# Two edits to an mLSTM and two-layer feed-forward kernel: who writes the opening's constant tiles, and where the second layer's weight decoding stands in VectorE's queue

## The chip, the cores and the metric

One core of a Trainium2 chip runs the whole program. The metric is the device time of one execution in microseconds (us). A profiled execution gives, besides its own time, a span: from the first to the last instruction of the trace. PE is TensorE's matmul side and PEld its weight loads, DVE is VectorE, ACT is ScalarE, POOL is GpSimd, and SP is the engine that only issues transfers (DMA).

## The reference

An mLSTM runs over 768 steps for 2 batches of 8 heads of width 40. Its output, 1536 tokens of 320 features, goes through two feed-forward layers of width 2048.

```python
m_new = np.maximum(f_gate[:, :, t] + m, i_gate[:, :, t])
f_stab, i_stab = np.exp(f_gate[:, :, t] + m - m_new), np.exp(i_gate[:, :, t] - m_new)
C = f_stab * C + i_stab * np.einsum('bhd,bhe->bhde', vt, kt)
n = f_stab * n + i_stab * kt
h_tilde = np.einsum('bhde,bhe->bhd', C, qt)
y[:, :, t] = sigmoid(o_gate) * h_tilde / np.maximum(np.abs(n . q), 1.0)

x = y.reshape(1536, 320)
h = x @ w_in;   x   = (h - np.tanh(h)) @ w_out        # first layer
h = x @ w_in2;  out = (h * np.tanh(softplus(h))) @ w_out2   # second layer (Mish)
```

The inputs are float32, except the weights, which come 64 bits wide and are decoded on the chip; the matrix products are made from a high and a low part of each operand.

## The kernel before, in words

**Tiling.** The 1536 tokens are 12 pieces of 128 (`order`: six chunks of each batch). The first layer takes them as 6 blocks of 2 pieces, the second as 3 blocks of 4. The hidden width 2048 is 16 slices `f` of 128. A tile of the first layer is a block and two slices, a tile of the second a block and one slice, so each is 512 columns wide. There are 48 tiles of either.

**A tile of the first layer.** `mm1` makes `h` in PSUM (L504, 16 matmuls of 256 columns), in one of three buffers of `ps_h`. `tile1` makes the activation: ACT takes two tanh, a square and a relu (L527, L528, L529, L532), DVE multiplies (`u*h`, L530), subtracts (`h-t`, L531, the last reader of the PSUM buffer) and merges (L533). `split_g` makes a high part on ACT (L143) and a low part on POOL (L517). `mm2` then adds to the accumulators of the block, 12 matmuls of 320 columns (L563, L564, L565); it stands two tiles behind `mm1`. At the end of a block's half DVE adds the accumulators into `xo` (L580).

**A tile of the second layer.** L504 makes 8 matmuls of 512 columns; ACT applies Mish twice (L544, L545) and DVE subtracts for the low part (L546, in `tile2`); then the same 12 matmuls.

**Decoding.** `conv_w(layer, f)` turns a raw weight slice into a high and a low part: DVE L180, DVE L181, ACT L182, DVE L184, ACT L187, and DVE L189 and L190 (on POOL for the first two slices). Raw slices of 704 KB are loaded by SP (L163) into three buffers; a load waits until the decoding of the slice that lay in the buffer before has ended with L190. `lead2` asks for the decodings of the second layer: the first four during the first layer's last tiles, each further one as the second layer's tiles go.

**What sets the order.** The program states an order, and a scheduler with a timing model then arranges each engine's queue; whatever it may run early it may put ahead of its place. On the chip each engine works its queue strictly in that order. `with after(x)` is the means to forbid it: an instruction traced in it stands behind those instructions of the list `x` that run on its own engine. The list `mark` holds instructions of the latest tile: in `tile1` the DVE product L530, in `tile2` the first Mish L544 on ACT alone. `lead2` traces its decodings behind `mark`.

**The opening.** Before the first weights are needed, `program` makes constant tiles: `sds` (two 128x128 indicator matrices) and `md_` (128x1024, entries 0 and -1), which the later chunks use as matmul operands for the gates, `Cst` (two state tiles of zeros), `identr` and the mask `cm`. POOL sets them (lines 621 to 648). In the same time DVE works on the gates (`gates`, L405 to L427 for the first chunk, the same scans again for the rest), ACT rounds the gate rows (`nr`, L143) and takes the exponentials of the first two chunks (`Dm`, L312), and PE multiplies the gates out (`nb`, L293 to L303) after a run of 14 matmuls (L603) that only keep it busy. Then ACT loads the sigmoid table for the output gates (L230), the exponential table again (L659), and the first decodings begin.

Of the kernel before, what the change touches and what calls it, by code (L numbers as in the profile page):

```python
# [8 lines left out]
F32 = mybir.dt.float32  # L9
F32R = mybir.dt.float32r  # L10
U32 = mybir.dt.uint32
AF = mybir.ActivationFunctionType
ALU = mybir.AluOpType
# [12 lines left out]
def kernel(  # L26
# [11 lines left out]
    nc = tc.nc  # L38
    B, P, _, HG, S = qk.shape
    H, L = 2 * HG, 128  # L40
# [5 lines left out]
    D1 = D + 1  # L46
# [42 lines left out]
    def pool(stack, name, bufs, side="left", **kw):  # L89
        return stack.enter_context(tc.tile_pool(name=name, bufs=bufs, side=side, **kw))  # L90
# [15 lines left out]
    once = pool(left, "once", 1)  # L106

    ident = const.tile([P, P], F32, name="ident")
# [11 lines left out]
    K0, KD = 2 * B, 2 * B + 2 * H  # L120
    sds = [once.tile([P, P], F32R, name=f"sd{b}") for b in range(B)]
    md_ = once.tile([P, 2, HG, L], F32R, name="md")
    dec = once.tile([P, B, HG, NCH], F32, name="dec")

    Cst = [once.tile([P, HG, 2, D1], F32, name=f"C{b}") for b in range(B)]

    last, chain, fill, mark, second = [], [], [], [], []
# [7 lines left out]
    def after(x):  # L135
        e = ExitStack()
        for i in x:
            e.enter_context(tc.issue_after(i.ins))
        return e

    def copy_r(eng, o, x):
        if eng == 0:
            nc.scalar.activation(out=o, in_=x, func=AF.Copy)  # L143
        elif eng == 1:
            nc.vector.tensor_copy(o, x)
        else:
            nc.gpsimd.tensor_scalar(o, in0=x, scalar1=1.0, scalar2=0.0, op0=ALU.mult, op1=ALU.add)
# [236 lines left out]
    identr, cm = part[:, 0], part[:, 1]  # L384
# [152 lines left out]
    def tile2(i):  # L537
        l, bi, f = tiles[i]
        nt = len(blk[l, bi]) * L
        h = hps.pop(i)  # L540
        p = late["B"]
        gh, gl = (p.tile([P, M2], F32R, tag=t, name=t, bufs=NG2)[:, 0:nt] for t in ("gh", "gl"))
        g = p.tile([P, M2], F32, tag="g2", name="g2", bufs=2)[:, 0:nt]
        mark[:] = [nc.scalar.activation(out=gh, in_=h, func=AF.Mish)]  # L544
        nc.scalar.activation(out=g, in_=h, func=AF.Mish)  # L545
        nc.vector.tensor_tensor(gl, in0=g, in1=gh.bitcast(F32), op=ALU.subtract)  # L546
        gs[i] = (gh, gl)

    def mm2(i):
# [46 lines left out]
    def program():  # L596
# [16 lines left out]
        for x in "qkqkOwOw":  # L613
# [7 lines left out]

        big = cm.bitcast(F32)
        nc.gpsimd.memset(big, 0.0)
        masked = nc.gpsimd.affine_select(
            out=cm, in_=big, pattern=[[1, L]], base=0, channel_multiplier=-1, compare_op=ALU.is_ge, fill=2.0 ** 100
        )

        for b, t in enumerate(sds):
            f = t.bitcast(F32)
            with after([masked]):  # L630
                nc.gpsimd.memset(f, 0.0)
            nc.gpsimd.affine_select(
                out=t, in_=f, pattern=[[0, P]], base=-b, channel_multiplier=1, compare_op=ALU.not_equal, fill=1.0
            )
            nc.gpsimd.affine_select(
                out=t, in_=f, pattern=[[0, P]], base=-B - b, channel_multiplier=1, compare_op=ALU.not_equal, fill=1.0
            )
        with after([masked]):
            nc.gpsimd.memset(md_.bitcast(F32), 0.0)
        mf = md_.bitcast(F32)  # L640
        for n in range(2):
            nc.gpsimd.affine_select(
                out=md_, in_=mf, pattern=[[-HG, 2], [-1, HG], [0, L]], base=-K0 - H * n, channel_multiplier=1,
                compare_op=ALU.not_equal, fill=-1.0,
            )
        with after([masked]):
            for t in Cst:
                nc.gpsimd.memset(t, 0.0)
        copy_r(0, identr, ident)
        for n, v_ in enumerate((-G_T,)):  # L650
            nc.vector.memset(bias[:, n:n + 1], v_)
        nc.vector.memset(ones, 1.0)
# [107 lines left out]
        seg_at, k = {}, 0  # L760
# [21 lines left out]
        for i in range(len(tiles)):  # L782
            l, bi, f = tiles[i]
            if i == n_s:
                fill.clear()
            if l == 0 and i in seg_at:
                k = seg_at[i]
# [21 lines left out]
            if l == 0:  # L809
                tile1(i)  # L810
                if not i:
                    session(2, NCH)
                qm.append(i)
                if len(qm) > LAG:
                    mm2(qm.pop(0))
                if i:
                    ahead(int(14 * (k + (i - i0 + 1) / n_seg + 0.4)))
                if k >= T2:
                    next(sg, None)
                    next(sg, None)  # L820
            else:
                tile2(i)
                qm.append(i)
                if len(qm) > LAG2:
                    mm2(qm.pop(0))
                next(sg, None)
        while qm:
            mm2(qm.pop(0))

    ones = const.tile([BH, HP], F32, name="ones")  # L830
    program()


# [59 lines left out]
```

## Time and profile before

| | |
|---|---|
| median of 3 runs | 472.6 us (472.59 to 474.25) |
| the profiled execution | 472.48 us, of which the trace's span is 470.4 us |
| mean granted TensorE clock | 0.992 |
| PE busy | 455.7 us (97% of the span) |
| weight loads | 412.7 us (88%) |
| DVE busy | 321.7 us (68%) |
| ACT busy | 284.1 us (60%) |
| POOL busy | 121.2 us (26%) |

The busy shares of the page tell where the work is. The 40 slices of the page, 11.8 us each, tell where PE has holes and where its granted clock fell. The chain of waits tells which engine the end depends on in each stretch. The timeline lists instructions in order of time, with the idle time before one and what ended it in brackets. PE's matmuls are pipelined and their ends are modelled, so its idle time is best read as the distance of two starts less the usual distance for so many matmuls.

### The profile page before, as it was taken

What the parts mean: (1) busy time and instruction counts of PE and PEld (TensorE: products, weight loads), DVE (VectorE), ACT (ScalarE), POOL (GpSimd) and SP (SyncE); (2) the same over time, 40 slices, a digit from 0 to 9 for tenths busy, and PEclk for the clock granted to TensorE, in tenths of its full rate; (3) what the DMA queues carried; (4) which work ended last, traced back from release to release, by engine and by line L of the source; (5) the groups of instructions that cost most, each with busy time, mean ns of one, the idle gap of its engine ahead of it and who ended that gap; (6) DMA issues with size and microseconds to landing.
All of it is one profiled execution on the core that took longest, in us unless ns stands there. A gap on an engine that the chain in (4) does not pass through costs nothing.

```text
span 470.4 us, 8021 instructions
## 1 busy us (share of the span) xinstructions
PE 455.7 (97%) x3103; PEld 412.7 (88%) x3103; DVE 321.7 (68%) x544; ACT 284.1 (60%) x513; POOL 121.2 (26%) x132
## 2 busy tenths in 40 slices
PE   9969989999999999999999998999999999999996
PEld 5636879999989999999999887999989888998995
DVE  8998999989876888666889887899942211221111
ACT  2979646685674865888887675877643323332331
POOL 9412536355363331342433333000000000000000
PEclk9997999999999999999999999999999999999999
DMA  7784462613505121000120110255301000010001
GB/s 246 269 325 128 143 190 81 216 49 109 156 5 173 35 63 63 1 1 1 63 63 0 63 57 7 75 176 181 123 1 56 2 0 1 0 57 0 1 0 56
DMA packets 22745, 38.04 MB, mean 81 GB/s; under 512 B 1364, under 2 KB 17044, under 8 KB 22708
## 3 DMA queue, kind: packets, MB, share of 16 engines
q1 hardware_dynamic: 22708, 37.54, 24.3%
q8 instruction: 24, 0.39, 0.4%
q14 instruction: 13, 0.11, 0.1%
HBM read 35.41 MB, written 1.97 MB: 79 GB/s over the span
## 4 chain that ended last, share of the span: by engine, by line
PE 74%; DVE 11%; issue 6%; ACT 4%; DMA 2%; POOL 2%; ACTq 0%; DVEq 0%; POOLq 0%; SPq 0%
PE h L504 32%; PE acc L563 10%; PE acc L565 10%; PE acc L564 10%; PE sc L329 4%; PE pv L349 3%; POOL gl L517 2%; DMA raw<-in_w_dram 2%; PE it L338 1%; PE xt L254 1%; DVE raw L181 1%; DVE raw L180 1%; PE st L370 1%; DVE g L530 1%; DVE t L531 1%
## 5 line engine op out<-in xcount | busy, mean ns | idle before, releaser
L504 PE MATMUL h<-xT,w 128*128 128x256 f32 (+1 forms) x1152 | 212.2, 324 | 7.1 <-ACT w L187 2.3
L504 PEld LDWEIGHTS h<-xT,w 128*128 128x128 f32 x1152 | 169.7, 190 | 24.8 <-ACT w L187 2.8
L563 PE MATMUL acc<-w,gh 128*128 128x320 f32 x384 | 119.4, 313 | 1.2 <-ACT gh L143 0.6
L564 PE MATMUL acc<-w,gh 128*128 128x320 f32 x384 | 118.0, 309 | 0.0
L565 PE MATMUL acc<-w,gl 128*128 128x320 f32 x384 | 109.9, 311 | 0.0
L517 POOL TENSOR_TENSOR gl<-g,gh 128x512 fp32r<-128x512 f32 x48 | 66.0, 1375 | 140.9 <-ACT gh L143 129.6
L546 DVE TENSOR_TENSOR gl<-g,gh 128x512 fp32r<-128x512 f32 x48 | 33.1, 690 | 85.7 <-ACT g L545 85.7
L563 PEld LDWEIGHTS acc<-w,gh 128*128 128x128 f32 x384 | 72.2, 188 | 5.0 <-issue 1.3
L544 ACT ACTIVATE gh<-h 128x512 fp32r<-128x512 f32 x48 | 28.6, 597 | 75.7 <-PE h L504 75.6
L564 PEld LDWEIGHTS acc<-w,gh 128*128 128x128 f32 x384 | 72.2, 188 | 2.1
L565 PEld LDWEIGHTS acc<-w,gl 128*128 128x128 f32 x384 | 69.5, 188 | 1.8 <-issue 0.4
L533 DVE COPY_PREDICATED g<-u,t 128x512 f32<-128x512 uint32 x48 | 41.0, 853 | 7.7 <-ACT u L532 7.5
L143 ACT ACTIVATE gh<-g 128x512 fp32r<-128x512 f32 x48 | 30.4, 633 | 23.8 <-DVE g L533 20.2
L530 DVE TENSOR_TENSOR g<-u,h 128x512 f32<-128x512 f32 x48 | 32.6, 680 | 16.1 <-ACT u L529 9.5
L532 ACT ACTIVATE u<-u,bias 128x512 f32<-128x512 f32 x48 | 34.8, 725 | 9.4 <-DVE g L530 9.2
L527 ACT ACTIVATE u<-h 128x512 f32<-128x512 f32 x48 | 28.3, 591 | 16.1 <-PE h L504 16.1
L187 ACT ACTIVATE w<-raw 128x704 fp32r<-128x704 f32 x32 | 27.5, 866 | 15.1 <-DVE raw L184 15.0
L184 DVE SCALAR_TENSOR_TENSOR raw<-raw 128x704 uint32<-128x704 uint32 x32 | 32.2, 1009 | 2.8 <-ACT raw L182 2.6
L182 ACT ACTIVATE raw<-raw 128x704 f32<-128x704 f32 x32 | 27.5, 864 | 10.0 <-DVE raw L181 9.0
L531 DVE TENSOR_TENSOR t<-h,t 128x512 f32<-128x512 f32 x48 | 32.8, 683 | 0.0
L529 ACT ACTIVATE u<-u 128x512 f32<-128x512 f32 x48 | 30.4, 634 | 0.0
L181 DVE SCALAR_TENSOR_TENSOR raw<-raw 128x704 uint32<-128x704 uint32 x32 | 30.0, 940 | 0.3
(105 smaller groups left out, 506.1 us busy)
## 6 DMA issues: line engine op xcount, KB each, us to landing
raw<-in_w_dram SPq DMA_DIRECT2D x32, 704.0 KB
qk_t<-in_qk_dram SPq DMA_DIRECT2D x12, 512.0 KB
kv_t<-in_kv_dram SPq DMA_DIRECT2D x12, 324.0 KB
out_dram<-xo SPq DMA_DIRECT2D x12, 160.0 KB
xo<-in_og_dram SPq DMA_DIRECT2D x2, 640.0 KB
xo<-in_og_dram SPq DMA_DIRECT2D x2, 320.0 KB
sd<-nr SPq DMA_DIRECT2D x20, 4.0 KB
md<-nr SPq DMA_DIRECT2D x10, 8.0 KB
```

Of the source, the lines that this page charges most:

```text
L181: nc.vector.scalar_tensor_tensor(lo32, in0=z, scalar=0x80000000, in1=lo32, op0=ALU.bitwise_and, op1=ALU.bitwise_or)
L184: third[layer, f] = nc.vector.scalar_tensor_tensor(z, in0=z, scalar=3, in1=lo32, op0=ALU.logical_shift_left, op1=ALU.bitwise_or)
L504: y = nc.tensor.matmul(t[:, k * nt:(k + 1) * nt], lhsT=w[:, o:o + P], rhs=x[:, kk, :], start=(n == 0), stop=(n == len(pairs) - 1),)
L517: nc.gpsimd.tensor_tensor(gl, in0=g, in1=gh.bitcast(F32), op=ALU.subtract)
L530: mark[:] = [nc.vector.tensor_tensor(g, in0=u, in1=h, op=ALU.mult)]
L531: nc.vector.tensor_tensor(t, in0=h, in1=t, op=ALU.subtract)
L532: nc.scalar.activation(out=u, in_=u, func=AF.Relu, bias=bias[:, 0:1])
L533: nc.vector.copy_predicated(out=g, mask=u.bitcast(U32), data=t)
L546: nc.vector.tensor_tensor(gl, in0=g, in1=gh.bitcast(F32), op=ALU.subtract)
L563: nc.tensor.matmul(a, lhsT=gh[:, sl], rhs=wh, start=(f in ends_), stop=False)
L564: nc.tensor.matmul(a, lhsT=gh[:, sl], rhs=wl, start=False, stop=False)
L565: nc.tensor.matmul(a, lhsT=gl[:, sl], rhs=wh, start=False, stop=(f + 1 in ends_ or f == NF - 1))
```

## The change

The constant tiles of the opening are no longer set by POOL. DVE adds columns of the identity matrix into `picks` (two short additions), and ACT copies a column of it over each tile (`sds`, and `md_` with scale -1); the zeros of `Cst` are copied by ACT from a constant. In `tile2` the list `mark` also gets DVE's subtraction L546, so that a decoding of the second layer that `lead2` traces behind a second-layer tile stands behind that tile's L546 in DVE's queue, as it did behind L544 in ACT's.

```diff
     def tile2(i):
         mark[:] = [nc.scalar.activation(out=gh, in_=h, func=AF.Mish)]
         nc.scalar.activation(out=g, in_=h, func=AF.Mish)
-        nc.vector.tensor_tensor(gl, in0=g, in1=gh.bitcast(F32), op=ALU.subtract)
+        mark.append(nc.vector.tensor_tensor(gl, in0=g, in1=gh.bitcast(F32), op=ALU.subtract))
...
-        masked = nc.gpsimd.affine_select(
+        nc.gpsimd.affine_select(
             out=cm, in_=big, pattern=[[1, L]], base=0, channel_multiplier=-1, compare_op=ALU.is_ge, fill=2.0 ** 100
         )
+        picks = once.tile([P, H + B, 1], F32, name="picks")
+        for n, (k, d, w_) in enumerate(((K0, H, H), (0, B, B))):
+            nc.vector.tensor_tensor(
+                picks[:, H * n:H * n + w_, 0], in0=ident[:, k:k + w_], in1=ident[:, k + d:k + d + w_], op=ALU.add
+            )
+        copy_r(0, identr, ident)
+        nc.scalar.activation(
+            out=md_.rearrange("p r g s -> p (r g) s"), in_=picks[:, 0:H].to_broadcast([P, H, L]), func=AF.Copy, scale=-1.0
+        )
         for b, t in enumerate(sds):
-            f = t.bitcast(F32)
-            with after([masked]):
-                nc.gpsimd.memset(f, 0.0)
-            nc.gpsimd.affine_select(out=t, in_=f, ...)
-            nc.gpsimd.affine_select(out=t, in_=f, ...)
-        with after([masked]):
-            nc.gpsimd.memset(md_.bitcast(F32), 0.0)
-        mf = md_.bitcast(F32)
-        for n in range(2):
-            nc.gpsimd.affine_select(out=md_, in_=mf, ...)
-        with after([masked]):
-            for t in Cst:
-                nc.gpsimd.memset(t, 0.0)
-        copy_r(0, identr, ident)
+            copy_r(0, t, picks[:, H + b].to_broadcast([P, P]))
+        zero = nc.const_aps.tensor(0.0, [P, HG * 2 * D1], F32)
+        for t in Cst:
+            copy_r(0, t.rearrange("p g r d -> p (g r d)"), zero)
```

The queues move in two places. The first is the start of POOL's and of ACT's queue, in the opening (`C_98`, `C_99` are the state tiles, `n_101` holds `identr` and the mask, `sd_94`, `sd_95` and `md` are the indicators). POOL's:

```order
 L623 MEMSET n_101 128x128
 L624 AFFINE_SELECT n_101<-n_101 128x128
-L631 MEMSET sd_94 128x128
-L631 MEMSET sd_95 128x128
-L639 MEMSET md 128x1024
-L648 MEMSET C_98 128x328
-L648 MEMSET C_99 128x328
-L632 AFFINE_SELECT sd_94<-sd_94 128x128
-L632 AFFINE_SELECT sd_95<-sd_95 128x128
-L642 AFFINE_SELECT md<-md 128x1024
-L635 AFFINE_SELECT sd_94<-sd_94 128x128
-L635 AFFINE_SELECT sd_95<-sd_95 128x128
```

Eleven instructions (the last, a second L642, follows these) leave POOL between the mask and `dl`. ACT's queue in the same place:

```order
 L609 ACT_TABLE_LOAD
 L609 ACTIVATE scr<-const-float32-0.0 128x1
+L143 ACTIVATE C_98<-const-float32-0.0 128x328
+L143 ACTIVATE C_99<-const-float32-0.0 128x328
 L143 ACTIVATE n_101<-ident 128x128
+L634 ACTIVATE md<-picks 128x1024
+L143 ACTIVATE sd_94<-picks 128x128
+L143 ACTIVATE sd_95<-picks 128x128
 L312 ACTIVATE Dm<-nb 128x512 x2
```

Five copies come in ahead of the first exponentials. PE's queue and SP's are the same in the opening, and DVE's gets the two short additions before its wait for the first gate rows.

The second place is DVE's queue at the end of the first layer. Before, the last tiles of that layer stand like this; `raw_3513` is the raw slice f=6 of the second layer, and `g_3340`, `g_3383` and `g_3430` are the activations of the last three tiles:

```order
L531 TENSOR_TENSOR t_3339<-h_3321,t_3339 128x512
L180 TENSOR_SCALAR raw_3513<-raw_3513 128x704
L533 COPY_PREDICATED g_3340<-u_3338,t_3339 128x512
L530 TENSOR_TENSOR g_3383<-u_3381,h_3364 128x512
L531 TENSOR_TENSOR t_3382<-h_3364,t_3382 128x512
L181 SCALAR_TENSOR_TENSOR raw_3513<-raw_3513 128x704
...
L533 COPY_PREDICATED g_3383<-u_3381,t_3382 128x512
L530 TENSOR_TENSOR g_3430<-u_3428,h_3411 128x512
L531 TENSOR_TENSOR t_3429<-h_3411,t_3429 128x512
L533 COPY_PREDICATED g_3430<-u_3428,t_3429 128x512
L546 TENSOR_TENSOR gl_3500<-g2_3501,gh_3499 128x512
L184 SCALAR_TENSOR_TENSOR raw_3014<-raw_3014 128x704
```

In the changed program the last two tiles of the layer are `g_3368` and `g_3415`, and the raw slices f=4, 5 and 6 are `raw_2999`, `raw_3212` and `raw_3498`:

```order
L533 COPY_PREDICATED g_3368<-u_3366,t_3367 128x512
L580 SCALAR_TENSOR_TENSOR xo_91<-acc_3292,xo_91 128x256
L580 SCALAR_TENSOR_TENSOR xo_91<-acc_3292,xo_91 128x128
L533 COPY_PREDICATED g_3415<-u_3413,t_3414 128x512
...
L546 TENSOR_TENSOR gl_3485<-g2_3486,gh_3484 128x512
L180 TENSOR_SCALAR raw_2999<-raw_2999 128x704
L546 TENSOR_TENSOR gl_3510<-g2_3511,gh_3509 128x512
L180 TENSOR_SCALAR raw_3212<-raw_3212 128x704
L181 SCALAR_TENSOR_TENSOR raw_2999<-raw_2999 128x704
L546 TENSOR_TENSOR gl_3535<-g2_3536,gh_3534 128x512
L180 TENSOR_SCALAR raw_3498<-raw_3498 128x704
```

The first two passes (L180, L181) of the slices f=4, 5 and 6 of the second layer stood among the first layer's tiles (those of `raw_3014` and `raw_3227` further ahead than the rows show) and now stand behind the first second-layer subtractions L546. With them the scheduler has arranged the matmuls of PE and the passes of ACT in that stretch anew; the work is the same.

## Rows read from the trace of the kernel before

**Rows 1.** Chain of waits, opening: start, length (us), engine, tile, line.

```profile
3.73 1.20 DVE n L410
...
5.56 1.06 DVE n L427
...
8.98 0.99 DVE gg L412
...
11.56 0.74 ACT nr L143
...
13.08 1.09 ACT Dm L312 x2
...
63.12 0.41 PE xt L254 x2
```

**Rows 2.** Timeline, opening: start, busy us, instruction, count, idle before it.

```profile
3.28 0.96 POOL L639 MEMSET md<- 128x1024 f32 x1
3.34 0.28 DVE L408 TENSOR_TENSOR gi<-gi,gF 16x128 f32<-16x128 f32 x1
...
8.06 1.28 ACT L312 ACTIVATE Dm<-nb 128x512 f32<-128x512 f32 x2 [5.57 <-PE nb L303]
...
8.19 1.75 POOL L642 TENSOR_SCALAR_AFFINE_SELECT md<-md 128x1024 fp32r<-128x1024 f32 x1
...
11.60 0.45 PE L303 MATMUL nb<-n 128*128 128x512 f32 x1
```

**Rows 3.** Timeline of DVE, end of the first layer.

```profile
265.22 0.53 DVE L180 TENSOR_SCALAR raw<-raw 128x704 uint32<-128x704 uint32 x1 [1.15 <-DMA raw<-in_w_dram]
...
283.17 0.53 DVE L180 TENSOR_SCALAR raw<-raw 128x704 uint32<-128x704 uint32 x1 [2.13 <-DMA raw<-in_w_dram]
```

**Rows 4.** Chain of waits, second layer: PE's steady pace.

```profile
455.42 1.85 PE h L504 x8
...
459.04 1.85 PE h L504 x8
```

**Rows 5.** Timeline of PE, end of the first layer and first tiles of the second.

```profile
259.43 2.10 PE L504 MATMUL h<-xT,w 128*128 128x256 f32 x16
261.87 0.38 PE L563 MATMUL acc<-w,gh 128*128 128x320 f32 x1 [0.34 <-DVE xo L580]
...
267.28 0.30 PE L565 MATMUL acc<-w,gl 128*128 128x320 f32 x1
268.15 0.41 PE L563 MATMUL acc<-w,gh 128*128 128x320 f32 x1 [0.56 <-ACT gh L143]
...
271.80 0.31 PE L565 MATMUL acc<-w,gl 128*128 128x320 f32 x1
272.77 2.14 PE L504 MATMUL h<-xT,w 128*128 128x256 f32 x16 [0.66 <-DVE t L531]
275.00 0.39 PE L563 MATMUL acc<-w,gh 128*128 128x320 f32 x1
...
284.25 0.31 PE L565 MATMUL acc<-w,gl 128*128 128x320 f32 x1
285.68 2.05 PE L504 MATMUL h<-xT,w 128*128 128x512 f32 x8 [1.11 <-DVE t L531]
287.90 0.39 PE L563 MATMUL acc<-w,gh 128*128 128x320 f32 x1 [0.17 <-DVE xo L580]
```

**Rows 6.** Timeline of DVE, second layer: decodings.

```profile
301.17 0.29 DVE L190 TENSOR_TENSOR w<-raw,w 64x128 fp32r<-64x128 f32 x1
...
306.03 0.90 DVE L181 SCALAR_TENSOR_TENSOR raw<-raw 128x704 uint32<-128x704 uint32 x1
...
312.27 0.29 DVE L190 TENSOR_TENSOR w<-raw,w 64x128 fp32r<-64x128 f32 x1
...
342.84 0.29 DVE L190 TENSOR_TENSOR w<-raw,w 64x128 fp32r<-64x128 f32 x1
```

**Rows 7.** Timeline of PE, second layer: last matmuls of slice f=4.

```profile
303.62 1.32 PE L504 MATMUL h<-xT,w 128*128 128x512 f32 x5
```

More of the change, by code (lines that the diff above doesn't have):

```diff
@@ L623, in program @@
         nc.gpsimd.memset(big, 0.0)
-        masked = nc.gpsimd.affine_select(
+        nc.gpsimd.affine_select(
             out=cm, in_=big, pattern=[[1, L]], base=0, channel_multiplier=-1, compare_op=ALU.is_ge, fill=2.0 ** 100
         )
-        for b, t in enumerate(sds):
-            f = t.bitcast(F32)
-            with after([masked]):
-                nc.gpsimd.memset(f, 0.0)
[L632 to L637, printed above, removed]
-        with after([masked]):
-            nc.gpsimd.memset(md_.bitcast(F32), 0.0)
-        mf = md_.bitcast(F32)
-        for n in range(2):
[L642 to L645, printed above, removed]
-        with after([masked]):
-            for t in Cst:
-                nc.gpsimd.memset(t, 0.0)
-        copy_r(0, identr, ident)
+        picks = once.tile([P, H + B, 1], F32, name="picks")
[7 more added lines that the diff above has]
+        )
+        for b, t in enumerate(sds):
+            copy_r(0, t, picks[:, H + b].to_broadcast([P, P]))
+        zero = nc.const_aps.tensor(0.0, [P, HG * 2 * D1], F32)
+        for t in Cst:
+            copy_r(0, t.rearrange("p g r d -> p (g r d)"), zero)
         for n, v_ in enumerate((-G_T,)):
```

## The prediction, made before the run

> **What bounds the kernel now.** I read the chain of waits first, because PE is busy in nearly the whole span and a busy share says nothing of which microsecond counts. The reader is to see that the chain has two kinds of stretch. From the first gate rows up to 63 us it runs through DVE and ACT alone, and only there does it pass to PE [rows 1]. PE is busy in that time too, but largely with fillers. So whatever shortens the DVE and ACT sequence before 63 us brings everything behind it forward. From 63 us to the end the chain is PE's, and there only a hole in PE's sequence costs time.
>
> For the holes I went to PE's timeline, since its idle brackets understate them: a matmul's modelled end covers part of a wait. In the second layer a tile takes 459.04 - 455.42 = 3.62 us, of which 1.85 for the h matmuls [rows 4]; the 12 matmuls into accumulators take the other 1.77, so 0.15 each. A first-layer h tile has 16 matmuls of half the width, the same columns, and so 1.85 as well. Distances between starts above this are lost. Six of them stand at the end of the first layer [rows 5]: 261.87 - 259.43 - 1.85 = 0.59; 268.15 - 267.28 - 0.15 = 0.72; 272.77 - 271.80 - 0.15 = 0.82; 275.00 - 272.77 - 1.85 = 0.38; 285.68 - 284.25 - 0.15 = 1.28; 287.90 - 285.68 - 1.85 = 0.37. Together 4.2 us. Gaps of about 0.1 at other changes between h and accumulators add up to some 0.8 more, an estimate. I found no such hole in the second layer until the last matmul.
>
> What ends these waits is DVE: t of L531, which frees an h buffer, the sums of L580, which free an accumulator, and g, from which ACT makes gh [rows 5]. And DVE itself, in the same stretch, sits idle in front of a decoding pass whose raw slice has not landed: 1.15 us before 265.22 and 2.13 us before 283.17 [rows 3]. Those slices are f=5 and f=6 of the second layer. DVE works its queue in order, so L533 and the next L530 and L531 stand still behind them.
>
> **The change, part by part.**
>
> *POOL loses eleven instructions in the opening.* Nothing waits for their results soon; what they cost is DVE's time. L410 took 1.20 us while POOL set md and the tiles behind it, L427 took 1.06, and L412, a copy of five columns, 0.99 while POOL's L642 ran [rows 1, 2]. DVE's L408, on as many elements as L410 and in the middle of POOL's memset of md, took 0.28 [rows 2]. I take 0.28 for each of the three without POOL: 0.92 + 0.78 + 0.71 = 2.4 us less on DVE until n_all is ready, 9.1 instead of 11.5. That is the upper bound of this part; nothing gained is the lower, in case the passes are slow for another reason.
>
> *What is late next.* ACT's two roundings nr began at 11.56 and lead to the Dm of the second piece at 13.08 [rows 1]. They would start when the first Dm ends, at 8.06 + 1.28 = 9.34 [rows 2], and take the same 13.08 - 11.56 = 1.52 us, until 10.9. But the second piece's Dm needs PE's last L303 of the gate products, which ends at 11.60 + 0.45 = 12.05 [rows 2], and PE gets there after a run of fillers and matmuls without a hole, which the change leaves alone. One exponential of a pair takes 1.28 / 2 = 0.64 or less, so the pair ends at about 12.65 instead of 13.08 + 1.09 = 14.17 [rows 1]. **Gain 1.5 us.** I take this value rather than 2.4 because the L303 row is a bound that stays. From there the sigmoid's table load, the sigmoids and the first decodings follow on ACT and DVE alone, so the 1.5 us should come through to 63 us. The loads that this sequence needs are issued by SP as their buffers come free, so they move with it.
>
> *ACT gains five copies, DVE two additions.* ACT waited 5.57 us before the first Dm [rows 2]; that is the cover. By the row, a 512-wide activation costs at most 0.64, so md (1024) costs at most 1.28, and the two state tiles and the two sd at most 0.64 each: 3.84, hidden with 1.7 us to spare. identr, which L303 needs, now stands behind the zeros, and so 1.28 us later at most, in the same wait. The additions go into DVE's wait for the gate rows. Cost: nothing. The Trainium skill speaks against this step: "ScalarE: Activation LUTs", Rules for kernel authors, gives additions and multiplications to VectorE rather than ScalarE, and its section on the table load puts an activation at 186 ns and 0.833 ns per column, by which the five would take an estimated 2.5 us. By that too they stay inside the wait; the rule matters only if the cover is gone, which is a rival below.
>
> *The second layer's early passes go behind L546.* In DVE's queue the first two passes of f=4, 5 and 6 leave the end of the first layer, and with them the two waits for a load of 1.15 and 2.13 us [rows 3] and three times 0.53 + 0.90 = 1.43 us of work [rows 3, 6], 4.3 us. With 1.15 + 2.13 + 4.3 = 7.6 us less in front of it, DVE's share of a tile (L530, L531, L533, L580) follows PE instead of holding it. Following the new order with the durations above, I find h buffers freed 2 to 4 us before PE asks, and no wait for gh or gl over a few tenths. The bounds: nothing gained, if the rearranged queues bring waits of their own, and 4.2 + 0.8 = 5.0, all of the holes. I take the six holes, **4.2 us**, and leave the small gaps, which are changes between kinds of matmul as much as waits.
>
> *What the moved work costs later.* DVE has the 4.3 us to do after the first L546. In the second layer POOL is idle and DVE nearly full: from the end of f=7 to that of f=15 eight decodings took 342.84 - 312.27 = 30.57 us, 3.82 each [rows 6], against PE's 3.62 [rows 4]. It lives on a lead. Before, f=4 was decoded at 301.17 + 0.29 = 301.46, and PE came for its low part at 303.62 [rows 6, 7], a lead of 2.2 us. After, DVE enters the layer sooner by what it no longer waits for; I count a lead of over 3 us at f=4 and about 2 at f=15. Cost: nothing, if that holds.
>
> **Sum.** The profiled execution took 472.48 us, 0.12 below the median of the three runs, 472.6. 472.48 - 1.5 - 4.2 = **466.8 us**, 1.2% under the median. About 0.5%, 2.4 us, can be told from no change here.
>
> **The rivals.**
> 1. *The opening gains nothing.* For it: PE's fillers are sized to this opening, and loads fill it. Against it: the chain of waits shows no transfer and no PE between the first Dm and 63 us. 472.48 - 4.2 = 468.3.
> 2. *Half of the head's gain is given back.* The new order runs two or three h tiles in a row and puts two tiles of DVE passes together; a wait for gl from POOL or for an accumulator can take the place of a wait for h. 472.48 - 1.5 - 2.1 = 468.9.
> 3. *The edit of mark brings nothing at the head*: the waits pass to the rearranged ACT queue. 472.48 - 1.5 = 471.0.
> 4. *PE waits for decodings in the second layer* (the other side). DVE enters the layer no sooner, because its last passes wait for ACT and for accumulators. Then f=4 comes 4.3 us later than before, 2.1 us after PE; and with no lead left each of the eleven slices f=5 to f=15 costs 3.82 - 3.62 = 0.2, 2.2 us. It decides from the point at which L190 of f=4 ends later than PE's first h matmul of f=4 plus four. With the opening's gain: 472.48 - 1.5 + 4.3 = 475.3.
> 5. *ACT is late with the copies.* If they took over 5.6 us, half as much again as the bound above, the first Dm moves: every us over is a us, and the opening's gain is gone after 1.5. At 1 us net loss, 472.48 + 1.0 - 4.2 = 469.3.
>
> **How the numbers follow.** The forecast has 0.56, rival 1 0.14, rival 2 0.12, rival 3 0.07, rival 4 0.09, rival 5 0.02. Faster by over 0.5% (under 470.2): the forecast and rivals 1, 2 and 5, 0.84, less 0.01 for their edge, 0.83. Rival 3 and a third of rival 4 with that edge make 0.11 for within 0.5%, and the rest of rival 4, 0.06, is slower (over 475.0). The forecast's own range is 465.2 (both parts nearly at their upper bounds, 0.9 and 0.8 more, would be 465.1) to about 468. To hold 8 in 10 the range must reach rivals 1 and 2: 465.2 to 469.6.
>
> **What would show it.** Opening: L410, L427 and L412 near 0.3 us, n_all ready near 9, the sigmoid's table load at about 12.7 instead of 14.2, and the chain's passage to PE near 61.6. If L410 stays over 1 us, the first step is wrong; if the table load comes earlier and 63 us does not, the way onward is. End of the first layer: no DVE idle in front of L180 among the tiles, and starts of PE there at 1.85 and 0.15 without holes. If holes remain, the engine named in front of them is rival 2 or 3. Second layer: L190 of f=4 ends over 2 us before PE needs it, and PE shows no wait for DVE or ACT on weights; if it does, rival 4. The forecast is wrong if the time lies over 468.5 with both mechanisms in place, for then PE was held by something that neither part names.

## The result, and the profile after

The changed kernel takes 469.01 us (median of 4 runs, 468.47 to 469.83) against 473.21 for the kernel before (4 runs beside them): ratio 0.9909, 95% interval 0.9886 to 0.9931, so 4.2 us or 0.9% faster. It lies inside the predicted range, 2.2 us above the predicted time. The profiled execution took 468.47 us, its span is 466.5 us (before: 472.48 and 470.4), at a mean granted clock of 0.991.

**Opening.** The timeline of DVE in the changed kernel (start, busy us, engine, instruction) answers to [rows 1]:

```profile
3.74 0.21 DVE L410 TENSOR_SCALAR n<-gi 16x128 fp32r<-16x128 f32 x1
...
4.89 0.28 DVE L427 TENSOR_TENSOR n<-n_all,n 32x128 fp32r<-32x128 f32 x1
...
7.46 0.15 DVE L412 COPY gg<-gF 16x5 f32<-16x5 f32 x1
7.65 1.54 DVE L413 TENSOR_TENSOR_SCAN n_all<-gg,n_all,gi 16x640 f32<-16x640 f32 x1
```

The three passes are short and n_all is ready at 9.19. ACT's timeline of the same stretch:

```profile
2.21 0.83 ACT L143 ACTIVATE C<-const-float32-0.0 128x328 f32<-128x328 f32 x2
...
3.14 1.04 ACT L634 ACTIVATE md<-picks 128x1024 fp32r<-128x1024 f32 x1
4.08 0.49 ACT L143 ACTIVATE sd<-picks 128x128 fp32r<-128x128 f32 x2
7.31 1.27 ACT L312 ACTIVATE Dm<-nb 128x512 f32<-128x512 f32 x2 [2.74 <-PE nb L303]
...
11.96 1.28 ACT L230 ACT_TABLE_LOAD   x1
```

The five copies take 2.4 us and leave 2.74 us of waiting before the first Dm, which begins earlier than before (7.31 against 8.06 in [rows 2]). The sigmoid's table load begins 2.2 us earlier. In ACT's timeline of the kernel before it stood behind the Dm of [rows 1]:

```profile
14.19 1.28 ACT L230 ACT_TABLE_LOAD   x1
```

In the changed kernel the chain of waits names a different engine at the start:

```profile
0.84 4.90 PE w_ps L603 x14
...
18.73 0.37 PE st L370 x9
...
20.40 0.86 ACT raw L182
...
61.26 0.41 PE xt L254 x2
```

PE's fillers head the chain now, and PE holds it until 19.1 us; then it runs through ACT and DVE, and it comes back to PE at 61.26, not 63.12 [rows 1]. So 1.9 us of the 2.2 arrive there.

**End of the first layer.** From 225 to 300 us DVE has no wait for a raw slice in front of L180, where it had 1.15 and 2.13 us [rows 3] and, for f=4 before 246.67, a further 1.31. Of PE's six holes [rows 5] none is left in its place; one new one has come, here in the timelines of PE, DVE and POOL:

```profile
266.51 3.62 PE L504 MATMUL h<-xT,w 128*128 128x256 f32 x29
270.96 0.39 PE L563 MATMUL acc<-w,gh 128*128 128x320 f32 x1 [0.83 <-DVE xo L580]
```

```profile
267.85 1.79 DVE L184 SCALAR_TENSOR_TENSOR raw<-raw 128x704 uint32<-128x704 uint32 x1
269.56 0.75 DVE L533 COPY_PREDICATED g<-u,t 128x512 f32<-128x512 uint32 x1
270.19 1.15 DVE L580 SCALAR_TENSOR_TENSOR xo<-acc,xo 128x256 f32<-128x256 f32 x4
```

```profile
267.59 1.30 POOL L517 TENSOR_TENSOR gl<-g,gh 128x512 fp32r<-128x512 f32 x1 [2.82 <-ACT gh L143]
```

29 matmuls of 1.85 / 16 each would be 3.35 us, and the next begins 4.45 after: 1.1 us lost. PE waits for an accumulator that L580 empties, and L580 stands behind the third pass L184 of a decoding, which takes 1.79 us in place of 0.88. That is about what is left of POOL's L517 when it begins (1.04, until 268.89) and then its own length, 1.92 together.

**Second layer.** PE now waits for weights, which it did not do before:

```profile
320.21 1.20 PE L504 MATMUL h<-xT,w 128*128 128x512 f32 x4 [0.23 <-ACT w L187]
...
331.92 1.20 PE L504 MATMUL h<-xT,w 128*128 128x512 f32 x4 [0.23 <-ACT w L187]
```

By the distance of starts these two lose 0.39 us each; two more before 324.18 and 335.91 lose 0.23 and 0.26. Together 1.3 us. DVE's timeline and the chain of waits say why:

```profile
297.07 0.29 DVE L190 TENSOR_TENSOR w<-raw,w 64x128 fp32r<-64x128 f32 x1
...
298.98 0.29 DVE L190 TENSOR_TENSOR w<-raw,w 64x128 fp32r<-64x128 f32 x1
...
301.50 0.53 DVE L180 TENSOR_SCALAR raw<-raw 128x704 uint32<-128x704 uint32 x1 [0.65 <-DMA raw<-in_w_dram]
...
305.14 0.53 DVE L180 TENSOR_SCALAR raw<-raw 128x704 uint32<-128x704 uint32 x1 [1.59 <-DMA raw<-in_w_dram]
305.59 0.89 DVE L184 SCALAR_TENSOR_TENSOR raw<-raw 128x704 uint32<-128x704 uint32 x1
...
309.48 0.29 DVE L190 TENSOR_TENSOR w<-raw,w 64x128 fp32r<-64x128 f32 x1
...
340.20 0.29 DVE L190 TENSOR_TENSOR w<-raw,w 64x128 fp32r<-64x128 f32 x1
```

```profile
299.35 5.77 DMA raw<-in_w_dram
```

The load of slice f=8 starts when the decoding of f=5 has left its buffer (298.98 + 0.29 = 299.27), takes 5.77 us, and DVE waits 1.59 us for it; L184 at 305.59, the next pass of f=7, stands behind that wait. In the kernel before, the same two slices waited too, but less, 0.73 us for f=7 and 0.41 for f=8:

```profile
303.34 0.29 DVE L190 TENSOR_TENSOR w<-raw,w 64x128 fp32r<-64x128 f32 x1
...
308.40 0.53 DVE L180 TENSOR_SCALAR raw<-raw 128x704 uint32<-128x704 uint32 x1 [0.41 <-DMA raw<-in_w_dram]
```

From the end of f=5 to L180 of f=8 were 308.40 - 303.63 = 4.77 us, and now are 305.14 - 299.27 = 5.87. Why this load is 1.1 us longer, no run shows; the loads of f=7, f=8 and f=9 overlap in both kernels. The lead of the decoding over PE, from the end of L190 to PE's matmuls on the low part, is seen in PE's timelines of the changed kernel (f=4, the first four of the eight matmuls, and f=7) and of the kernel before (f=7):

```profile
299.26 2.01 PE L504 MATMUL h<-xT,w 128*128 128x512 f32 x8
...
310.31 1.10 PE L504 MATMUL h<-xT,w 128*128 128x512 f32 x4
```

```profile
314.23 1.10 PE L504 MATMUL h<-xT,w 128*128 128x512 f32 x4
```

At f=4 it is 299.26 - 297.36 = 1.9 us (2.2 before), at f=7 310.31 - 309.77 = 0.5 us (314.23 - 312.56 = 1.7 before). From f=7 to f=15 a decoding takes (340.20 - 309.48) / 8 = 3.84 us, more than PE's 3.62 [rows 4], so the rest of the lead is soon gone; the first wait, at 320.21, is for f=10. The last decoding ends at 340.49, only 2.6 us earlier than before (342.84 + 0.29 in [rows 6]), while PE entered the layer nearly 5 us earlier (1.7 and 3.1 us, worked out in the point-by-point part).

### The profile page after: what moved, and what is told of

It is laid out like the page before. It is cut to its first block, busy times and chain, and to the rows that moved or that the text cites. A ratio compares the mean times of both kernels' runs of the same rounds, so it can differ in the third digit from the quotient of the medians.

```text
span 466.5 us, 8014 instructions
## 1 busy us (share of the span) xinstructions
PE 454.3 (97%) x3103; PEld 412.5 (88%) x3103; DVE 317.0 (68%) x546; ACT 286.7 (61%) x518; POOL 113.4 (24%) x121
## 3 DMA queue, kind: packets, MB, share of 16 engines
q1 hardware_dynamic: 22708, 37.54, 24.7%
## 4 chain that ended last, share of the span: by engine, by line
PE 69%; DVE 15%; issue 7%; ACT 5%; POOL 2%; DMA 1%; POOLq 0%; ACTq 0%; DVEq 0%; SPq 0%
PE h L504 28%; PE acc L565 9%; PE acc L563 9%; PE acc L564 9%; PE sc L329 4%; PE pv L349 4%; DVE raw L184 3%; POOL gl L517 2%; DVE raw L181 2%; DVE raw L180 2%; DVE gl L546 2%; PE it L338 2%; DVE w L189 1%; DVE w L190 1%; PE w_ps L603 1%
## 5 line engine op out<-in xcount | busy, mean ns | idle before, releaser
L563 PE MATMUL acc<-w,gh 128*128 128x320 f32 x384 | 118.4, 312 | 0.8 <-DVE xo L580 0.8
L565 PE MATMUL acc<-w,gl 128*128 128x320 f32 x384 | 108.7, 311 | 0.0
L517 POOL TENSOR_TENSOR gl<-g,gh 128x512 fp32r<-128x512 f32 x48 | 65.5, 1365 | 135.4 <-ACT gh L143 131.0
L546 DVE TENSOR_TENSOR gl<-g,gh 128x512 fp32r<-128x512 f32 x48 | 33.2, 691 | 87.1 <-ACT g L545 87.0
L544 ACT ACTIVATE gh<-h 128x512 fp32r<-128x512 f32 x48 | 28.7, 597 | 77.1 <-PE h L504 74.2
L563 PEld LDWEIGHTS acc<-w,gh 128*128 128x128 f32 x384 | 72.1, 188 | 3.3 <-ACT w L187 1.0
L527 ACT ACTIVATE u<-h 128x512 f32<-128x512 f32 x48 | 28.4, 593 | 16.6 <-PE h L504 16.6
L184 DVE SCALAR_TENSOR_TENSOR raw<-raw 128x704 uint32<-128x704 uint32 x32 | 32.2, 1006 | 3.1 <-ACT raw L182 3.0
L181 DVE SCALAR_TENSOR_TENSOR raw<-raw 128x704 uint32<-128x704 uint32 x32 | 28.7, 899 | 0.3
```

What stands on the lines that cost most here:

```text
L181: nc.vector.scalar_tensor_tensor(lo32, in0=z, scalar=0x80000000, in1=lo32, op0=ALU.bitwise_and, op1=ALU.bitwise_or)
L184: third[layer, f] = nc.vector.scalar_tensor_tensor(z, in0=z, scalar=3, in1=lo32, op0=ALU.logical_shift_left, op1=ALU.bitwise_or)
L517: nc.gpsimd.tensor_tensor(gl, in0=g, in1=gh.bitcast(F32), op=ALU.subtract)
L546: mark.append(nc.vector.tensor_tensor(gl, in0=g, in1=gh.bitcast(F32), op=ALU.subtract))
L563: nc.tensor.matmul(a, lhsT=gh[:, sl], rhs=wh, start=(f in ends_), stop=False)
L565: nc.tensor.matmul(a, lhsT=gl[:, sl], rhs=wh, start=False, stop=(f + 1 in ends_ or f == NF - 1))
```

## The experiments

Each ratio is to runs of the kernel before on the same chip. The changed kernel's own ratio is 0.9909.

### The two edits alone

`e_open`: the change without its line in `tile2`.

```diff
-        mark.append(nc.vector.tensor_tensor(gl, ...))
+        nc.vector.tensor_tensor(gl, ...)
```

> The kernel before with the edit of the opening alone; the queues of PE and SP are those of the kernel before. Theory: the opening is worth 1.5 us and up to 2.2 if PE's fillers finish as early as in the changed kernel's profile (5.7 us instead of 6.4). Sigmoid's table load at 12.0 to 12.7 instead of 14.19, everything at 63 us 1.2 to 1.9 earlier, of which 1.5 to 1.7 is left at 245 us; the six holes of PE at the end of the first layer (4.2 us) and DVE's two waits for raw slices stay. So 473.2 - 1.5 = 471.7 us, ratio 0.996 to 0.997. Rival A (the opening's gain is given back in the first layer, where PE already waits for DVE): 63 us earlier, 285 us not, 473 us. Rival B (the two edits help one another): the holes shrink too, since DVE has more lead, and the time is below 470.5 us.

Measured: 471.4 us, ratio 0.9968 (0.9956 to 0.998), so 1.5 us, with an interval from 0.9 to 2.1. The time is the theory's, and both rivals' times are out. Where the gain lies is not shown, because the profiled execution is the odd one of the last section, with PE at about half its pace; only DVE's opening can be read from it, and there L410, L427 and L412 take 0.21, 0.28 and 0.15 us as in the changed kernel.

`e_mark`: the kernel before with that line alone.

```diff
-        nc.vector.tensor_tensor(gl, ...)
+        mark.append(nc.vector.tensor_tensor(gl, ...))
```

> The kernel before with the edit of mark alone; the queues of PE and SP are those of the changed kernel, the opening is that of the kernel before (table load at 14.2). Theory: the rearranged end of the first layer saves about 3.3 us of PE's holes, and the second layer gives back 1.2 to 1.3 us in waits for weights decoded by ACT and DVE, in both cases whatever the opening does: 473.2 - 2.1 = 471.1 us, ratio 0.995 to 0.996. Its sum with the opening alone is then the whole change (-4.2). Rival A (the head's gain needs the lead that the opening gives DVE): within 0.8 us of before, above 472.4. Rival B (the waits in the second layer come from the opening being earlier, loads being too late): then they are absent here and the time is below 470.3 us.

Measured: 471.28 us, ratio 0.9967 (0.9955 to 0.9979), so 1.6 us. The table load stands at 14.19. The hole before L563 (0.83 in brackets, 1.09 lost) and the waits for weights (0.52, 0.26, 0.38, 0.26 us) are nearly those of the changed kernel, so neither depends on the opening; rivals A and B are out. The two parts by ratio give 0.9968 x 0.9967 = 0.9935 against 0.9909. The missing 1.2 us are no larger than the intervals of the three ratios together allow. But 1.0 us of them is in this profile. PE's timeline, and the table by stretch (busy us of PE, PEld, DVE, ACT and POOL with their instructions, then the granted clock, the DMA share and GB/s):

```profile
16.20 1.08 PE L349 MATMUL pv<-kv_t,Dm 128*128 128x41 f32 x8 [0.18 <-DVE Dm L331]
...
17.60 1.74 PE L349 MATMUL pv<-kv_t,Dm 128*128 128x41 f32 x8
```

```profile
15.00:20.00 5.00, 4.78 (x32) 3.48 (x32) 4.64 (x11) 4.20 (x7) 1.05 (x2) 0.78 0.66 181
20.00:25.00 5.00, 5.00 (x34) 2.25 (x33) 3.88 (x9) 3.33 (x8) 2.28 (x2) 0.53 1.05 403
```

PE came early (fillers of 4.83 us) and waited for DVE's Dm. Then the granted clock was 0.50, the 1.2 GHz level, from about 17.8 to 24.7 us (by the table 2.2 us of the first stretch and 4.7 of the second), and the same eight matmuls take 1.74 us instead of 1.08. The first tanh L527 begins at 31.24 against 30.26 in the profile before, 1.0 us late. From there on this kernel saves 2.0 us of the span (470.4 to 469.4), as the changed kernel does (3.9 us of the span, of which it has 1.9 by the first tanh, at 28.34).

### POOL beside DVE

`e_dead`: POOL works on an unread tile, in short instructions.

```diff
...
+        dead = once.tile([P, 2 * L], F32, name="dead")
+        with after([masked]):
+            for _ in range(8):
+                nc.gpsimd.memset(dead, 0.0)
+        for _ in range(9):
+            nc.gpsimd.affine_select(out=dead, in_=dead, pattern=[[0, 2 * L]], ...)
```

> The changed kernel with POOL kept busy again in the opening, by 8 memsets and 9 affine selects on a tile that nobody reads; the result does not change, and PE's and SP's queues are those of the changed kernel. Theory (it is POOL's work beside DVE that made the short DVE passes long): L410 back to 1.0 us or more, L427 too if an affine select runs beside it, n_all ready 1.5 us or more later than 9.19, the sigmoid's table load at 13.2 or later instead of 11.96, and the time 1.2 to 1.7 us above the changed kernel, about 470.4 us (ratio to before 0.994). Rival A (the passes were long because their operands came from POOL, or because of what ACT and PE did at the time): L410 and L427 stay at 0.2 to 0.3, the time stays at 469.0 us. Rival B (PE's fillers set the opening): the passes get long but the table load comes only 0.7 us later or less, and the time is within 0.7 us of the changed kernel.

Measured: 471.08 us (469.31 to 472.0), ratio 0.9954 (0.9939 to 0.9968). L410 took 0.30, L427 0.28, L412 0.36; the table load stood at 12.34, 0.4 us late. The theory as written missed. The time is over rival A's as well: in this profile PE waits 0.26 and 0.32 us for Dm near 16 and 17.5, and the granted clock is then 0.79 in 15 to 20 us and 0.53 in 20 to 25, as in `e_mark`. The eleven executions fall in two groups: four took 469.31 to 469.61 us at a mean granted clock of 0.989 to 0.991, seven took 470.89 to 472.0 at 0.983 to 0.989. The first group is within 0.6 us of the changed kernel's median, so what POOL's short instructions cost by themselves is small.

`e_dead3`: three memsets of 128x1024 in place of those seventeen.

```diff
...
+        dead = xp.tile([P, 2 * WC], U32, tag="x", name="dead", bufs=NB - 1).bitcast(F32)
+        with after([masked]):
+            for _ in range(3):
+                nc.gpsimd.memset(dead[:, 0:2 * HG * L], 0.0)
```

> The changed kernel with three memsets of 128x1024 put back on POOL behind the mask, on a tile that nobody reads; PE's and SP's queues and every other engine's are those of the changed kernel. The run before this one used short POOL instructions (256 columns), and L410 took only 0.30 us beside them. Theory (a DVE pass of the kinds of L410, L427 and L412 waits until the POOL instruction then running has ended, so that long POOL instructions cost and short ones don't): L410, which begins at 3.7 inside a memset of 0.96 us, ends with the end of a memset (3.9, 4.9 or 5.8 us), 0.5 to 2.1 us long; L427 too if it begins before 5.8; n_all ready 0.7 to 2 us later than 9.19; sigmoid's table load at 12.5 to 13.5 instead of 11.96. Time 0.5 to 1.5 us above the changed kernel's 469.0. Rival (long or short, POOL beside DVE costs nothing, and in the kernel before it was the operands that came late): L410 at 0.2 to 0.3, time 469.0.

Measured: 469.92 us, ratio 0.9944 (0.993 to 0.9958); table load at 12.83, which its fillers of 5.78 us explain (next group); n_all was ready at 9.36, only 0.2 us late, so the theory's size missed. DVE's passes, then POOL's:

```profile
3.72 0.29 DVE L410 TENSOR_SCALAR n<-gi 16x128 fp32r<-16x128 f32 x1
...
4.61 0.41 DVE L422 CAST n<-n_all 128x128 fp32r<-128x128 f32 x1
5.06 0.28 DVE L427 TENSOR_TENSOR n<-n_all,n 32x128 fp32r<-32x128 f32 x1
```

```profile
2.98 2.98 POOL L631 MEMSET dead<- 128x1024 f32 x3
```

The first two memsets end at 3.94 and 4.95. L410 ends at 4.01 and L422 (0.23 alone) at 5.02, each just behind one; L427, inside the third, is not held at all. In `e_dead` it is the same on a smaller scale: L410 ends at 4.10 behind a memset that ends at 4.03, and L412 at 7.89 behind a select that ends at 7.87. So a pass does wait for the end of a POOL instruction, but here only for the rest of one, and not every pass does. "SBUF — State Buffer" of the Trainium skill, in "SBUF: two separate sides", says that GpSimd and VectorE share a pair of ports, held by one for a whole instruction, and that a VectorE operation with two SBUF inputs is shut out only by a GpSimd operation that reads SBUF. The runs agree: L427 has two inputs, takes 0.28 inside a memset and 1.06 beside a select [rows 1].

`e_dead4`: all eleven old instructions, on an unread tile, with dl behind them.

```diff
...
-            copy_r(2, dl, Dm[:, :, L - 1:L])
+            with after(deads):
+                copy_r(2, dl, Dm[:, :, L - 1:L])
...
+            for n in (P, P, 2 * HG * L, HG * 2 * D1, HG * 2 * D1):
+                nc.gpsimd.memset(dead[:, 0:n], 0.0)
+        for n in (P, P, 2 * HG * L, P, P, 2 * HG * L):
+            deads.append(nc.gpsimd.affine_select(out=dead[:, 0:n], ...))
```

> The changed kernel with all eleven POOL instructions of the kernel before put back, in the old order and sizes (five memsets, six affine selects), but on a tile that nobody reads, and dl behind them. The scheduler arranges later tiles anew, so only the first 20 us are read. Theory (POOL's instructions beside DVE, memsets and above all affine selects, hold some DVE passes until the running POOL instruction ends, whoever reads the tiles): the old picture returns, L410 1.0 to 1.2 us, L427 about 1.0, L412 about 1.0, n_all ready at 11.5 and the sigmoid's table load at 14.2, 1.5 to 2.2 us later than in the changed kernel's profiles (11.96 to 13.0). Rival (the old passes waited on their operands, which shared a tile or a counter with what POOL wrote): the passes stay at 0.15 to 0.4 us as in the two runs with POOL work so far, and the table load at 12 to 13.

```profile
3.72 0.81 DVE L411 TENSOR_SCALAR n<-gi 16x128 fp32r<-16x128 f32 x1
...
13.40 1.28 ACT L230 ACT_TABLE_LOAD   x1
```

L410 (L411 here) is back at 0.81, L427 took 0.39, L412 0.25, n_all was ready at 10.74 and the table load came 1.4 us late. That lies between the theory and the rival. Of the 2.3 us that n_all moved from before to the changed kernel (11.53 to 9.19) 1.55 return, without anyone reading the tiles: POOL's work as such makes DVE late. But only half of the return is in the three passes of the prediction (0.60, 0.11 and 0.10 more than in the changed kernel). Most of the rest is in two others, L408 of the later chunks (1.48 against 0.81) and L422 (0.50 against 0.23). That L427 and L412 were long before for the same reason is not shown by this run; in the trace before, L412 ends at 9.97 [rows 1], 0.03 us behind POOL's select L642 [rows 2], as it does in `e_dead`. Why the other 0.8 us did not return is open. One difference is in the traces: before, each of POOL's instructions began before the last had ended (at 4.17, where the memset of md ends at 4.24 [rows 2]), and L410 ended at 4.93, behind the last memset (4.86); here they stand some 0.05 us apart, and L411 ended at 4.53, behind the memset that was running (4.46). (The whole, 478.35 us, is not compared: PE stands still for 1.94 us before 14.59, DVE makes the Dm that PE needs only from 13.81 on, behind L180 and L181 of a decoding, and the granted clock is 0.50 from 15 to 25 us.)

### PE's fillers

`before_again`: the kernel before, unchanged.

> The kernel before once more, for a second profile of it. In the profiles so far PE's 14 opening fillers took 4.83 to 4.90 us in three kernels and 5.65 or 5.66 in two others, with no order in it that follows the edits. Theory (this belongs to the execution, not to the kernel): the fillers may take either here; if 4.9, the first Dm begins near 7.3 instead of 8.06 but the sigmoid's table load stays at 14.19, set by DVE and ACT, PE waits for DVE's Dm of L331 between 15 and 18 us, and a granted clock under 1.00 follows, as with the edit of mark alone; the time is then 473.0 to 474.0 us. If 5.66, everything is as in the profile before, 472.4 to 472.8 us. Rival (the edit of the opening speeds the fillers up): they take 5.6 us or more here in any case and the time does not differ with it.

Measured: 472.77 us, fillers 6.12 us, table load 14.18. That is a third value, and with it ten profiles of kernels with these 14 fillers show 4.62 to 6.12 us, in no order of the edits: before 5.66, with the line in `tile2` alone 4.83, the changed kernel 4.90, `e_pool` 5.65. With the new opening and nothing added on POOL the table load follows them: 4.90 and 11.96, 5.65 and 12.71, 5.89 and 12.94, 5.96 and 13.00, always 7.04 to 7.06 apart. With the old one it is 14.18 or 14.19 at 4.83, 5.66 and 6.12. So the cap of the prediction is real, and the rival (the edit speeds the fillers up) is out, because the fillers are short in a kernel without that edit (4.83) and long in others with it (5.65 to 5.96).

`e_fill10`: the changed kernel with fewer fillers.

```diff
-        spin(14)
+        spin(10)
```

> The changed kernel with 10 fillers instead of 14 at PE's start; the scheduler arranges later parts of the queues anew. In the profiles with the new opening the sigmoid's table load stands at 11.96 where the fillers took 4.90 us and at 12.71 to 13.00 where they took 5.65 to 5.96. Theory (with DVE out of the way PE's fillers and gate products are the last to come, the cap of the prediction): with four fillers fewer PE is ready at 5.2, when L427 ends, and the table load comes at 11.9 to 12.2 whatever the clock; 0 to 1 us is gained, on average 0.5: 468.5 us. Rival A (with fewer fillers the clock rises later, and the gate products run at half speed): the table load at 12.5 or later, no gain. Rival B (the rearranged queues decide): the opening is earlier, but the time is over 469.5 us.

```profile
0.84 4.42 PE L603 MATMUL w_ps<-const-bfloat16-1.0 128*32 128x512 bf16 x10 [0.84 <-PEq L874]
```

The table load came at 11.78, as the theory says. But the exponential's load behind it came at 15.29, later than the 14.63 of the changed kernel, because ACT waits 0.72 us between the two sigmoids for the transfer of the output gates, which the changed kernel does not. At the first tanh (28.68 against 28.34) nothing was left. Three executions, with the profiled one, took 469.3, 469.44 and 471.52 us, ratio 0.9941 (0.9919 to 0.9962): no gain. Three more took 476.47 to 477.08 at a mean granted clock of 0.973, where the others had 0.985 to 0.996; no profile shows where the clock fell in them.

### The lead in the second layer

`e_pool`: the last two passes of f=7 to 15 on POOL.

```diff
-        eng = nc.gpsimd if layer == 0 and f < PRE else nc.vector
+        eng = nc.gpsimd if layer == 0 and f < PRE or layer == 1 and f >= 7 else nc.vector
```

> The changed kernel with L189 and L190 of the second layer's slices f=7 to 15 on POOL, which is idle there, instead of DVE; the queues up to the second layer stay. Theory (the 1.2 to 1.3 us that PE waits for weights at 319, 323, 331 and 335 us come from DVE's pace of 3.8 us for a decoding and its tile against PE's 3.62): DVE is relieved of 1.05 us in each, the waits go, and the time is 467.7 to 468.0 us, 1.0 to 1.3 us below the changed kernel. Rival A (the pace is set by the way back and forth between DVE and ACT or by the arrival of raw slices, 0.65 and 1.59 us of DVE's wait at 301 and 305 us): waits stay, 469.0 us. Rival B (POOL is slower at these passes than DVE, and DVE's own passes get longer beside them): weights come later, PE waits 2 us or more in all, above 470 us.

Measured: 474.39 us, ratio 1.004 (1.0026 to 1.0053): rival B, over 5 us worse than the changed kernel. Groups by line, 300 to 350 us:

```profile
L189 POOL TENSOR_TENSOR w<-raw,w 128x576 fp32r<-128x576 f32 x9 | 14.4, 1601 | 38.6 <-ACT w L187 35.8 <-issue 2.0 <-POOL w L190 0.7
...
L180 DVE TENSOR_SCALAR raw<-raw 128x704 uint32<-128x704 uint32 x9 | 8.8, 973 | 2.4 <-DMA raw<-in_w_dram 2.4
```

POOL needs 1.60 us for L189, DVE 0.76, and DVE's L180 grows from 0.52 to 0.97 beside it. PE loses 2.2 us before 327.63 and 2.0 before 342.17.

`e_E5`: five decodings in the first layer, one per three tiles.

```diff
-        CY, R2, E2 = 6, 4, 4
+        CY, R2, E2 = 6, 3, 5
```

> The changed kernel with one more decoding of the second layer asked for in the first layer's second halves (five instead of four, one per three tiles instead of four). Theory (the 1.2 to 1.3 us of waits for weights in the second layer are a lead that is 3.8 us per decoding too short at its end): f=4 is decoded in the first layer, the lead in the second is longer by one decoding, the waits at 319, 323, 331 and 335 us go, and the time is 467.7 to 468.2 us if the first layer, where DVE is 76% busy at 120 to 240 us, takes the extra decoding without new holes. Rival A (DVE's passes in the first layer push the tiles behind them again, or wait for raw slices among them as before the change): new holes of 1 us or more at 220 to 290 us, 469 to 471 us. Rival B (raw slices arrive no earlier, so the lead is not longer): the waits stay, 469.0 us.

Measured: 471.01 us, ratio 0.9961 (0.9947 to 0.9976): both at once. The waits for weights are gone, and the holes are back in the first layer (0.57 us before 243.91, 0.66 before 263.07, 0.65 before 275.62, with smaller ones), rival A.

`e_E5r4`: the fifth asked for at the last tile only.

```diff
-        CY, R2, E2 = 6, 4, 4
+        CY, R2, E2 = 6, 4, 5
```

> The changed kernel with the fifth decoding of the second layer asked for at the first layer's last tile instead of at the second layer's second, the pace of the first four as it is. Theory (a longer lead removes the waits for weights): f=4 is decoded about one tile earlier than in the changed kernel, by up to 3 us, the waits for weights in the second layer shrink from 1.3 us to 0.5 or less, and the time is 468.0 to 468.4 us. Rival (its first passes are again among the last tiles of the first layer and hold them up, the state before the change in small): holes of 0.5 us or more come back at 275 to 290 us, 469 to 470 us.

Measured: 468.75 us, ratio 0.9915 (0.9901 to 0.9928), over the theory's 468.0 to 468.4 and under the rival's 469. Its opening was 1.0 us later than the changed kernel's (fillers 5.96), its end 0.5: the longer lead gives back about 0.5 us of the 1.3, and waits for weights of some 0.6 us are left (0.29 before 315.93, 0.28 before 324.47). By the ratios the two kernels can't be told apart.

`e_fill10b`: `spin(10)` and E2 = 5 together.

> The changed kernel with 10 fillers and with the fifth decoding of the second layer asked for at the first layer's last tile, the combination of two single steps. The fifth decoding alone gave 468.75 us in executions whose opening was late (table load at 13.00 in the profile), with 0.5 us less at the end than at 28 us against the changed kernel. Theory: both add up, the table load at 11.9 to 12.2 and no waits for weights of over 0.5 us in the second layer, 467.6 to 468.2 us, ratio to before 0.990. Rival (the rearranged queues bring new holes at the end of the first layer): 469 us or more.

Measured: 468.66 us, ratio 0.9912 (0.9898 to 0.9926), over the theory's 467.6 to 468.2. The table load stands at 10.98, with fillers of 3.62 us, but ACT then waits 1.13 us for the output gates, and the first tanh begins at 28.28, where the changed kernel has it. Faster than before, not measurably faster than the changed kernel, so no version found beats both.

## Why the prediction was right or wrong, point by point

- **The three passes beside POOL: right.** 0.21, 0.28 and 0.15 us against the assumed 0.28, n_all at 9.19 against 9.1. That POOL's work as such makes DVE late is shown by `e_dead4`, for two thirds of the 2.3 us on n_all; in these three passes about a third came back there, most of it in L410.
- **Gain 1.5, capped by PE's L303: the cap is right, the size in part luck.** With fillers as in the profile before (5.65 us, `e_pool`) the table load comes at 12.71, against about 12.7 predicted. But not all of it comes through to 63 us: there PE's L254 begins 1.15 us earlier (61.97 against 63.12), and the first tanh of the 37th tile 1.0 (236.31 against 237.33). In the profiled execution of the changed kernel the fillers took 0.76 us less, which is nothing that the change did; the table load came 2.2 early, and 1.7 is left at the 37th tile (235.63). By its time `e_open` gives 1.5, without its fillers being known.
- **ACT's copies at nothing: right.** 2.4 us inside the wait. The estimate of 2.5 us from "ScalarE: Activation LUTs" of the Trainium skill agrees, and md with its 1024 columns took 1.04.
- **The six holes, 4.2 us: mis-sized.** They went, but a hole of 1.1 us came in their stretch: about 3.1. It is the mechanism of rival 2, a wait for an accumulator, at half its price. My walk through the new order took L184 at its length alone; it took 1.79 us beside POOL's L517.
- **"Cost: nothing, if that holds": the step that failed.** The lead did not hold, and PE lost 1.3 us for weights, rival 4 in small. I counted a lead of over 3 us at f=4 and about 2 at f=15. It was 1.9 at f=4, 0.5 at f=7, and used up at f=10. I let DVE enter the layer earlier by the waits it no longer had. But PE came earlier as well, at f=4 by 4.4 us (303.62 to 299.26) where DVE gained 4.1 (301.46 to 297.36), and loads are tied to decodings by three buffers, so the loads of f=7 to f=9 could not start before f=4 to f=6 were done. Before, f=7 ended 7.8 us behind f=6 (at 304.74 and, by [rows 6], 312.56); after, 8.9 us (300.85 and 309.77). These 1.1 us are the shrinking of the lead at f=7, and about what DVE's wait for the load of f=8 grew by (0.41 to 1.59). That PE lacked lead is supported by the two runs with an earlier fifth decoding: the waits for weights are gone in `e_E5`, where PE also came later, and about halved in `e_E5r4`.
- **Sum.** 472.48 - 1.7 - 3.1 + 1.3 = 469.0 with the measured terms, against 468.47 in the profiled execution; the 0.5 between is of the size of the small gaps that I had left out.
- **"Wrong if over 468.5 with both mechanisms in place":** the median is. What then held PE were things the text had named, an accumulator and weights, but as rivals. The median lies over the forecast's own range, to about 468, and inside the stated one, which was widened to reach rivals 1 and 2.

## What to carry to other kernels

When work is moved to remove a wait for a load, follow the buffers: the load waits for the buffer's last reader, so the wait moves with the work, and the lead must be counted from there. Moving short setup work off POOL can shorten passes of DVE that never read it. Before giving a queue's slack to POOL, price both sides: POOL's pass and DVE's passes beside it.

## What the runs showed of the hardware that was not expected

The same 14 matmuls at the start took 4.62 to 6.12 us in ten executions: two starts are 0.43 us apart at first and 0.22 later, and the step comes at another time in each, in three of them not before the last filler, while the granted clock column reads 1.00 there. A wait of 0.2 to 0.3 us near 16 us was followed in two kernels by some 7 us at a granted clock of 0.50, the 1.2 GHz level. No run shows that the wait is the cause; if it is, DVE's lateness in an opening is dearer than its own length. And one execution of `e_open` took 882.5 us: PE is busy 99% of a span of 880.6, its matmuls L563 take 0.50 us on average against 0.31 in the changed kernel, and the reported clock is 1.000. It looks like half speed from end to end; nothing in that profile says why.
